# Pieces of x sent from ACT's queue, and the first weight tiles asked for ahead of unit 1's loads

## The chip, the cores and the metric

One core of a Trainium2 chip. The metric is the device time of one execution in microseconds; the kernel before takes 977.13 us (median of 3 runs, 976.09 to 979.07).

## What is computed

A gated linear attention over 4 batches, 8 heads, 768 steps and heads of 48, then two MLPs, from 384 to 2048 and back, over the 3072 tokens:

```python
state = zeros((B, H, D, D))
for t in range(S):
    state = alpha[:, :, t, :, None] * state + einsum('bhd,bhe->bhde', k[:, :, t], v[:, :, t])
    y[:, :, t] = einsum('bhd,bhde->bhe', q[:, :, t], state)
x = y.transpose(0, 2, 1, 3).reshape(B * S, H * D)      # 3072 x 384
h = x @ w_in1
x = where(h >= 1, h, where(h <= -1, 0, (h + 1) ** 2 / 4)) @ w_out1
h = x @ w_in2
out = (h * cos(h)) @ w_out2
```

The weights are float64, read as pairs of 32-bit words. The kernel rebuilds a float32 from each pair and splits it in a high and a low fp32r half.

## The kernel before, in words

**Tiling.** The tokens form 8 units of 384 (half a batch each), the heads 4 pairs. `attention(m)` handles one pair of one unit (32 in all), in chunks of 128 steps; pair 3 of a unit comes first, then 0, 1 and 2. It loads alpha, k and q ("token loads", line 465 for units 0 and 1, line 473 for later ones) and v (line 431 for unit 0, line 492 later), turns them (TensorE for units 0 and 1, line 531; DVE later, line 519), scans alpha forward and backward on DVE (lines 561 and 593), makes masked scores (lines 689 and 699), chunk states (`ks` copied by ACT at line 653 or carried through DRAM, the outer products at line 721, scaled by ACT at line 782 into `kf` and `T`, advanced by DVE at line 792) and y (lines 746 and 751). ACT writes the high half of the result (`high`, line 830), DVE or for four pairs POOL the low half (lines 844 and 838).

**The pieces of x.** The MLP wants 384 rows as 3 tiles of 128, but a pair has 2 x 48 rows in a tile. The result of the first pair of a unit goes to a staging tile `stg`; from there pieces of 16 rows, two transfers for each of the other three pairs, are sent into the free rows of their tiles (`fragments`, line 852). That makes 24 pairs of transfers, 48 KB each, and all of them are issued by SP. `step1` of a unit waits for them.

**The weights.** `weight(layer, kind, f)` fetches a raw tile (lines 326, 329, 339 and 340), then ACT scales (line 352, `wy`), DVE rebuilds (lines 356, 360 and 366, `wz`), ACT makes the high half (line 377) and POOL the low one (line 381). In layer 1 two tiles of w_in are fetched together, 288 + 96 KB twice, and a tile of w_out is 384 KB. Raw buffers: two slots for pairs of w_in, two for w_out. 32 tiles of layer 1 are kept in SBUF, and all units use them.

**The MLPs.** `step1` does for a unit and one of the 16 slices of 128 hidden columns: h (9 matmuls, line 888) into one of two `h` banks, relu by ACT (line 966, or lines 978 to 984), two operations by DVE (lines 970 and 974, or 992), the high half of g by ACT (line 919), its low half by POOL (line 924), and 9 matmuls into acc. `step2` does the same with h cos h. In the units 0 and 1 the turning of tokens uses the `h` banks too.

**What sets the order.** `Order` is a planner that runs while the kernel is built. Every operation is added with its engine, an assumed duration, the operations that it comes after, its buffers, a latency `lat` for those behind it and a `span` that counts in its priority (its `tail`: the longest sum of spans behind it; without a `span` the duration counts). The planner takes the engine whose next operation can start first by its own model, and of those ready at that time the one with the largest tail. It emits the instructions in that order, and each engine runs its own in order. SP and ACT are engines among the others: an issue of a transfer takes its place in the queue of the engine that it is given to, with its wait. `SPREAD` gives the pairs' results a span.

Of the kernel before, what the change touches and what calls it, by code (L numbers as in the profile page):

```python
# [37 lines left out]
Q_DVE = (0, 1, 2, 3, 4, 6)  # L38
TURN = 2
MERGED = 0  # L40
LOW_POOL = (25, 28, 30, 31)
ALPHA_BANK = "sc"
ACT_STEPS = ((4, 10, 12, 15), (1, 4, 10, 14))
# [23 lines left out]
class Order:  # L67
# [7 lines left out]
    def buf(self, tag):  # L75
        b = Buf(tag)
        b.seq = self.made[tag] = self.made.get(tag, -1) + 1
        return b

    def add(self, eng, dur, fn, after=(), new=(), use=(), span=None, lat=None):  # L80
        lat = LATENCY.get(eng, 0.0) if lat is None else lat
        op = Op(len(self.ops), eng, dur, fn, [], list(new), dur if span is None else span, lat)
        for b in new:
            b.first = op
        for b in (*new, *use):
            b.users.append(op)
        op.after = list({id(x): x for x in (*after, *(b.first for b in use)) if x is not None}.values())
        for x in op.after:
            x.next.append(op)
        op.need = len(op.after)  # L90
        self.ops.append(op)
        return op
# [64 lines left out]
def gla_two_mlps(  # L157
# [21 lines left out]
    nc = tc.nc  # L179
# [3 lines left out]
    NP = H // 2  # L183
# [37 lines left out]
    add, buf = o.add, o.buf  # L221
# [5 lines left out]
    def dve(n):  # L227
        return n / 960 + 0.07
# [4 lines left out]
    def pool(n):  # L233
        return n / 960 * 2.5 + 0.04 if n > 100 else n / 400 + 0.1
# [7 lines left out]
    HW2, HW3, SWDMA, LOAD = 0.475, 0.65, 1.02, 2.0  # L242
# [44 lines left out]
    pair_of = {}  # L287

    def weight(layer, kind, f, after=()):
# [15 lines left out]
        new = not joint or f % 2 == 0  # L305
        rb = buf(tag) if new else pair_of["buf"]
# [76 lines left out]
        hb, lb = buf(f"w{kind}hi"), buf(f"w{kind}lo")  # L383
        if new:
            cost = 3.4 if joint else 1.6
            pair_of["op"] = add("sp", cost, fetch, after, new=[rb], lat=LOAD + 1)
        a = pair_of["op"]
        a = add("act", act(n, 0.09), scale, [a], new=[yb], use=[rb])
        a = add("dve", dve(n), shift, [a], new=[zb], use=[yb])
# [3 lines left out]
        lo = add("pool", pool(n), rest, [hi], new=[lb], use=[zb, hb])  # L393
# [6 lines left out]
    X1OPS = {}  # L400
# [6 lines left out]
    v0_ops = []  # L407
    v0b = buf("x2_0")
    chain = [None]

    def early_buffers():

        for _ in range(2):
            xb, t = buf("x"), {}

            def take(t=t):
                t[0] = xp.tile([P, 8, 2, CH * D], F32, tag="x", name="raw0")

            add(None, 0.0, take, new=[xb], lat=0.0)
            xraw.append((xb, t))  # L420
        add(None, 0.0, None, new=[v0b], lat=0.0)
        b, t = buf("x2_2"), {}

        def take_second():
            t[0] = x2p.tile([P, 6, N], F32, tag="x2_2", name="second")

        add(None, 0.0, take_second, new=[b], lat=0.0)
        xraw.append((b, t))
        for c in range(CH):
            def load(c=c):  # L430
                nc.sync.dma_start(
                    v0[:, c, :, 0:D], v[0, :, c * C:(c + 1) * C, :].rearrange("h p d -> p h d")
                )
            v0_ops.append(add("sp", 1.0, load, use=[v0b], lat=LOAD + 1))

    def attention(m):
        u, j = pairs[m]
# [13 lines left out]
        loads, rawb = [], []  # L451
        for x, src in enumerate((alpha, k, q)):
            i = 3 * m + x
            in_x = turned and i < 16
            rb = xraw[i // 8][0] if in_x else buf("raw")

            def load_tokens(x=x, src=src, i=i, rb=rb, in_x=in_x):

                if in_x:
                    dst = xraw[i // 8][1][0][:, i % 8]  # L460
                else:
                    dst = raw_b[rb.slot][:, 0:2 * CH * D].rearrange("p (e x) -> p e x", e=2)
                d["raw", x] = dst.rearrange("p e x -> p (e x)")
                off = ((b * H + 2 * j) * S + s0) * D
                nc.sync.dma_start(dst, bass.AP(src.tensor, off, [[CH * D, P], [S * D, 2], [1, CH * D]]))

            def load(e, z, x=x, src=src, rb=rb):

                d["raw", x] = dst = raw_b[rb.slot]
                off = ((b * H + 2 * j + e) * S + s0) * D + 32 * z  # L470
                n = R * D - 32 * z
                p0 = 64 * e + 32 * z
                nc.sync.dma_start(dst[p0:p0 + 32, 0:n], bass.AP(src.tensor, off, [[R * D, 32], [1, n]]))  # L473

            if not in_x:
                add(None, 0.0, None, new=[rb], lat=0.0)
            if turned:
                loads.append([add("sp", 0.7, load_tokens, use=[rb], lat=LOAD)])
            else:
                loads.append([  # L480
                    add("sp", HW2, lambda e=e, z=z, f=load: f(e, z), use=[rb], lat=LOAD)
                    for e in range(2) for z in range(2)
                ])
            rawb.append(rb)
# [252 lines left out]
        def within_and_before(cs):  # L737

            def fn():
                if cs[0] == 0:  # L740
                    yb.tile = ps(tag_y)
                for c in cs:
                    s = slice(c * C, (c + 1) * C)
                    t = state[c][0]
                    for e, z in enumerate((slice(0, 64), slice(64, K))):
                        nc.tensor.matmul(  # L746
                            yb.tile[z, s], lhsT=vcols(c, z), rhs=am_b[amb.slot][:, e, s], start=True, stop=t is None
                        )
                    if t is not None:
                        for e, z in enumerate(hrows):  # L750
                            nc.tensor.matmul(  # L751
                                yb.tile[z, s], lhsT=state_of(t)[:, e, :], rhs=d["tq"][0:K, s], start=False, stop=True
                            )

            known = [x for c in cs for x in state[c] if x is not None]
            done.append(
                add(
                    "pe",
                    0.15 + 0.235 * sum(1 if state[c][0] is None else 2 for c in cs),
                    fn,  # L760
                    [*masks, *v_ops[:cs[-1] + 1], *(x for x in known if isinstance(x, Op))],
                    new=[yb] if cs[0] == 0 else [],
                    use=[amb, vb, qb, *(x for x in known if isinstance(x, Buf))] + ([yb] if cs[0] else []),
                )
            )

        for c in range(CH):
            start = s0 == 0 and c == 0
            state[c] = (None, None) if start else (T[j], T_OP[j])
            if u < MERGED:  # L770
                within_and_before([c])
# [36 lines left out]
        first, late = j == NP - 1, early and j == NP - 2  # L808
# [5 lines left out]
        xb, stb = X1B[u]  # L814
# [33 lines left out]
        def fragments(js):  # L848
            def fn():
                for jj in js:  # L850
                    for i in range(2):
                        nc.sync.dma_start(
                            x1["x"].bitcast(F32)[64 * i + D:64 * i + 64, jj],
                            x1["stg"].bitcast(F32)[64 * i + 16 * jj:64 * i + 16 * jj + 16],
                        )
            return fn
# [8 lines left out]
            new=[stb] if first else [xb] if makes else [],  # L865
            use=[yb] + ([] if first or makes else [xb]),
        )
        if m in LOW_POOL:
            ycb = buf("ta")
            a = add("act", act(N), copied, [hi], new=[ycb], use=[yb])  # L870
            lo = add("pool", k_ * pool(N), low_pool, [a], use=[ycb, stb if first else xb])
        else:
            lo = add("dve", k_ * dve(N), low, [hi], use=[yb, stb if first else xb])
        X1OPS[u].append(lo)
        X1OPS.setdefault((u, "first"), lo)
        if early and first:
            add(None, 0.0, new_x1, new=[xb], lat=0.0)
            X1OPS[u].append(add("sp", 2 * HW3, fragments([NP - 2]), [lo], use=[xb, stb], lat=LOAD))
        elif not first and not late:
            X1OPS[u].append(add("sp", 2 * HW3, fragments([j]), [lo, X1OPS[u, "first"]], use=[xb, stb], lat=LOAD))  # L880
        chain[0] = add(None, 0.0, None, [X1OPS[u][-1], None if first else chain[0]], span=SPREAD.get(u, SPREAD[None]), lat=0.0)
        X1OPS[u].append(chain[0])
        GLA_END.append(lo)
# [262 lines left out]
    steps = [(u, f, f == a, f == b - 1, a > 0) for u, a, b in segs for f in range(a, b)]  # L1146

    early_buffers()
    for m in range(len(pairs)):
        attention(m)  # L1150
    judge()
    for f in range(FT):
        weight(1, "in", f)
        weight(1, "out", f)
    for s in steps:
        step1(*s)
    for f in range(FT):
        weight(2, "in", f, after=GLA_END[-1:])
        weight(2, "out", f, after=GLA_END[-1:])
# [195 lines left out]
```

## Time and profile before

| | |
|---|---|
| median of 3 runs | 977.13 us (976.09 to 979.07) |
| profiled execution | 979.92 us, its span 978.1 us |
| TensorE busy | 943.6 us (96%) |
| DVE busy | 592.0 us (61%) |
| ACT busy | 580.9 us (59%) |
| POOL busy | 427.1 us (44%) |
| mean granted TensorE clock | 0.993 of full speed |
| transfers | all issued by SP, 70.62 MB on its queue |

The engines' busy time counts no issue of a transfer; these stand in the rows of the queues (SPq). Matmuls are pipelined and their ends are modelled, so a busy TensorE is not at its peak all the time. A wait is put down to the one that came last. The attention of all units and the first MLP fill the span until about 500 us, the second MLP the rest.

### The profile page before, as it was taken

The numbers are of one execution on the slowest core, as the hardware profiler recorded it, in microseconds if no ns is written. First come the engines' busy times: TensorE is split into PE (matmuls) and PEld (weight loads), VectorE is DVE, ScalarE is ACT, GpSimd is POOL, SyncE is SP. The second block draws the span as 40 slices with busy tenths as digits, with TensorE's granted clock in tenths as the row PEclk, the third lists the DMA queues.
The fourth block names the chain that finished last, engine by engine and source line by source line (L and its number), as shares of the span: only waits on it lengthen the run. The fifth ranks groups of instructions, "written<-read, shape, count | busy, mean of one in ns | idle before, by whom it ended". The sixth has DMA issues, their size and how long they took to land.

```text
span 978.1 us, 17438 instructions
## 1 busy us (share of the span) xinstructions
PE 943.6 (96%) x6186; PEld 902.2 (92%) x6186; DVE 592.0 (61%) x1237; ACT 580.9 (59%) x1318; POOL 427.1 (44%) x464
## 2 busy tenths in 40 slices
PE   7779989999999999999999999999999999999997
PEld 5658878899999999989999999999999999999996
DVE  5789899788868677676446896333333333333332
ACT  3657666544545444544445698666666666666664
POOL 2246565555334334443336686434342434243322
PEclk9899999999999999999999999999999999999999
DMA  7677585334645334342132451000000000000000
GB/s 163 126 166 146 140 178 133 76 76 110 138 99 108 91 76 113 74 115 52 21 118 79 133 160 34 25 1 25 1 25 1 25 1 25 1 25 1 25 1 28
DMA packets 113552, 71.82 MB, mean 73 GB/s; under 512 B 71728, under 2 KB 96304, under 8 KB 113456
## 3 DMA queue, kind: packets, MB, share of 16 engines
q1 hardware_dynamic: 113456, 70.62, 30.5%
q8 instruction: 50, 0.82, 0.4%
q14 instruction: 46, 0.38, 0.1%
HBM read 58.79 MB, written 9.44 MB: 70 GB/s over the span
## 4 chain that ended last, share of the span: by engine, by line
PE 84%; DVE 6%; DMA 3%; ACT 2%; issue 2%; SPq 2%; POOL 0%; DVEq 0%; POOLq 0%; ACTq 0%
PE acc L888 33%; PE h L888 27%; PE sc L888 5%; PE kv L888 5%; PE y L888 5%; PE y L746 2%; PE sc L689 2%; PE h L531 2%; PE y L751 1%; PE kv L721 1%; DVE wz L356 1%; DMA raw<-in_alpha_dram 1%; DMA w_raw<-in_moe_w_in_dram 1%; SPq L473 1%; DMA ks<-scr 1%
## 5 line engine op out<-in xcount | busy, mean ns | idle before, releaser
L924 POOL TENSOR_TENSOR gl<-ang,gh 128x384 fp32r<-128x384 f32 x127 | 128.8, 1014 | 233.9 <-ACT gh L919 208.4
L924 POOL TENSOR_TENSOR gl<-r,gh 128x384 fp32r<-128x384 f32 x128 | 131.8, 1030 | 172.1 <-ACT gh L919 138.0
L888 PE MATMUL h<-x,winhi 128*128 128x384 f32 x768 | 198.6, 339 | 6.2 <-DVE r L974 3.1
L888 PEld LDWEIGHTS h<-x,winhi 128*128 128x128 f32 x768 | 137.8, 188 | 10.4 <-DVE r L974 3.9
L888 PE MATMUL acc<-gh,wouthi 128*128 128x384 f32 x384 | 135.8, 354 | 0.0
L888 PE MATMUL acc<-gl,wouthi 128*128 128x384 f32 x384 | 130.0, 338 | 0.3 <-POOL gl L924 0.3
L888 PE MATMUL acc<-gh,woutlo 128*128 128x384 f32 x384 | 130.0, 339 | 0.0
L888 PE MATMUL h<-x,winlo 128*128 128x384 f32 x384 | 129.0, 336 | 0.6 <-POOL winlo L381 0.5
L966 ACT ACTIVATE r<-h,half 128x384 f32<-128x384 f32 x120 | 69.7, 581 | 96.7 <-PE h L888 95.7
L970 DVE TENSOR_TENSOR h<-r,h 128x384 f32<-128x384 f32 x120 | 67.3, 561 | 83.6 <-ACT r L966 83.2
L919 ACT CAST gh<-r 128x384 fp32r<-128x384 f32 x128 | 65.6, 512 | 79.4 <-DVE r L974 71.6
L1077 ACT ACTIVATE ang<-ang 128x384 f32<-128x384 f32 x128 | 67.2, 525 | 61.8 <-DVE ang L1072 61.8
L888 PE MATMUL h<-x2s,winhi 128*128 128x384 f32 x402 | 103.0, 337 | 0.0
L919 ACT CAST gh<-ang 128x384 fp32r<-128x384 f32 x128 | 65.7, 513 | 55.8 <-DVE ang L1084 55.8
L888 PE MATMUL acc<-wouthi,gl 128*128 128x384 f32 x288 | 97.4, 338 | 0.3 <-POOL gl L924 0.3
L888 PE MATMUL acc<-wouthi,gh 128*128 128x384 f32 x288 | 96.9, 337 | 0.0
L888 PE MATMUL acc<-woutlo,gh 128*128 128x384 f32 x288 | 96.9, 336 | 0.0
L1084 DVE SCALAR_TENSOR_TENSOR ang<-ang,h 128x384 f32<-128x384 f32 x67 | 37.1, 554 | 67.6 <-ACT ang L1080 67.5
L888 PEld LDWEIGHTS acc<-gh,wouthi 128*128 128x128 f32 x384 | 71.9, 187 | 6.5 <-issue 2.8
L888 PEld LDWEIGHTS h<-x2s,winhi 128*128 128x128 f32 x402 | 73.4, 188 | 0.0
L888 PEld LDWEIGHTS h<-x,winlo 128*128 128x128 f32 x384 | 72.1, 188 | 1.2 <-POOL winlo L381 1.2
L888 PEld LDWEIGHTS acc<-gl,wouthi 128*128 128x128 f32 x384 | 72.1, 188 | 0.8 <-POOL gl L924 0.8
(167 smaller groups left out, 2118.7 us busy)
## 6 DMA issues: line engine op xcount, KB each, us to landing
w_raw<-in_moe_w_out_dram SPq DMA_DIRECT2D x18, 384.0 KB, 3.4
scr<-G SPq DMA_DIRECT2D x96, 48.0 KB, 1.8
ks<-scr SPq DMA_DIRECT2D x24, 192.0 KB, 2.7
out_dram<-o SPq DMA_DIRECT2D x24, 192.0 KB, 1.9
v<-in_v_dram SPq DMA_DIRECT2D x56, 72.0 KB, 2.6
w_raw<-in_moe_w_in_dram SPq DMA_DIRECT2D x10, 384.0 KB, 3.5
raw<-in_alpha_dram SPq DMA_DIRECT2D x48, 72.0 KB, 2.1
raw<-in_k_dram SPq DMA_DIRECT2D x48, 72.0 KB, 2.0
```

Of the source, the lines that this page charges most:

```text
L356: nc.vector.tensor_scalar(out=t["z"], in0=t["y"], scalar1=3, scalar2=None, op0=ALU.logical_shift_left)
L473: nc.sync.dma_start(dst[p0:p0 + 32, 0:n], bass.AP(src.tensor, off, [[R * D, 32], [1, n]]))
L531: nc.tensor.transpose(bank.tile[0:n, c:N:CH], d["raw", x][:, f0:f0 + n], ident)
L689: nc.tensor.matmul(x.tile[:, s], lhsT=d["tk"][z, s], rhs=d["tq"][z, s], start=True, stop=True)
L746: nc.tensor.matmul(yb.tile[z, s], lhsT=vcols(c, z), rhs=am_b[amb.slot][:, e, s], start=True, stop=t is None)
L888: nc.tensor.matmul(o, lhsT=lhs[a], rhs=rhs[b], start=first and i == 0, stop=last and i == 2)
L919: nc.scalar.copy(ghb.tile, g())
L924: eng.tensor_tensor(out=glb.tile, in0=g(), in1=ghb.tile, op=ALU.subtract)
L966: nc.scalar.activation(rb.tile, h.tile[:, 0:N], AF.Relu, bias=half, scale=0.5)
L970: nc.vector.tensor_tensor(out=hh, in0=rb.tile, in1=hh, op=ALU.max)
L1077: nc.scalar.activation(rb.tile, rb.tile, AF.Sin, scale=HALF_TURN)
L1084: nc.vector.scalar_tensor_tensor(out=rb.tile, in0=rb.tile, scalar=1.0, in1=h.tile[:, 0:N], op0=ALU.subtract, op1=ALU.mult)
```

## The change

The pieces of x are sent by ACT's queue instead of SP's (`nc.scalar.dma_start`), and the planner has them as operations of ACT of twice 0.475 us (`HW2`) instead of twice 0.65 us on SP. Three kinds of loads get a larger span: the fetches of the first w_in pair and of the first two w_out tiles (`f < W_SOON` in layer 1), and unit 0's v loads 4000 more, and the token loads of the first four pairs (unit 0) 8000 more. The durations and latencies of the loads stay as they are.

```diff
+SOON = 4000.0
+W_SOON = 2
+U_SOON = 4
...
             cost = 3.4 if joint else 1.6
-            pair_of["op"] = add("sp", cost, fetch, after, new=[rb], lat=LOAD + 1)
+            pair_of["op"] = add(
+                "sp", cost, fetch, after, new=[rb], span=cost + SOON * (layer == 1 and f < W_SOON), lat=LOAD + 1
+            )
...
-            v0_ops.append(add("sp", 1.0, load, use=[v0b], lat=LOAD + 1))
+            v0_ops.append(add("sp", 1.0, load, use=[v0b], span=1.0 + SOON, lat=LOAD + 1))
...
             if turned:
-                loads.append([add("sp", 0.7, load_tokens, use=[rb], lat=LOAD)])
+                loads.append([add("sp", 0.7, load_tokens, use=[rb], span=0.7 + 2 * SOON * (m < U_SOON), lat=LOAD)])
...
                 for jj in js:
                     for i in range(2):
-                        nc.sync.dma_start(
+                        nc.scalar.dma_start(
                             x1["x"].bitcast(F32)[64 * i + D:64 * i + 64, jj],
                             x1["stg"].bitcast(F32)[64 * i + 16 * jj:64 * i + 16 * jj + 16],
                         )
...
         if early and first:
             add(None, 0.0, new_x1, new=[xb], lat=0.0)
-            X1OPS[u].append(add("sp", 2 * HW3, fragments([NP - 2]), [lo], use=[xb, stb], lat=LOAD))
+            X1OPS[u].append(add("act", 2 * HW2, fragments([NP - 2]), [lo], use=[xb, stb], lat=LOAD))
         elif not first and not late:
-            X1OPS[u].append(add("sp", 2 * HW3, fragments([j]), [lo, X1OPS[u, "first"]], use=[xb, stb], lat=LOAD))
+            X1OPS[u].append(add("act", 2 * HW2, fragments([j]), [lo, X1OPS[u, "first"]], use=[xb, stb], lat=LOAD))
```

## Rows read from the trace of the kernel before

**Rows 1.** The page's busy times: us, share of the span, instructions.
```profile
PE 943.6 (96%) x6186; PEld 902.2 (92%) x6186; DVE 592.0 (61%) x1237; ACT 580.9 (59%) x1318; POOL 427.1 (44%) x464
```
**Rows 2.** Stretches: length, busy PE, PEld, DVE, ACT, POOL; clock, DMA share, GB/s.
```profile
0.00:10.00 10.00, 5.14 (x23) 4.08 (x24) 3.65 (x12) 2.89 (x6) 4.46 (x24) 1.00 0.92 185
10.00:20.00 10.00, 9.47 (x70) 7.42 (x70) 6.05 (x18) 3.95 (x13) 1.29 (x3) 1.00 0.75 185
20.00:30.00 10.00, 8.79 (x98) 7.10 (x99) 8.03 (x22) 5.89 (x18) 1.26 (x3) 1.00 0.69 125
30.00:67.00 37.00, 27.20 (x290) 22.66 (x287) 28.46 (x78) 24.19 (x67) 12.13 (x14) 0.86 0.64 136
67.00:120.00 53.00, 49.23 (x324) 45.06 (x325) 47.11 (x93) 34.22 (x82) 33.23 (x33) 1.00 0.71 150
120.00:200.00 80.00, 74.00 (x494) 67.20 (x492) 69.24 (x137) 49.94 (x116) 44.83 (x45) 1.00 0.54 120
200.00:500.00 300.00, 298.64 (x2217) 279.01 (x2217) 214.05 (x475) 143.88 (x357) 125.27 (x141) 1.00 0.40 89
```
**Rows 3.** Groups of instructions, 0 to 200 us: DVE's rebuilding of the weights.
```profile
L356 DVE TENSOR_SCALAR wz<-wy 128x384 int32<-128x384 int32 x32 | 19.9, 636 | 1.7 <-ACT wy L352 1.6
L360 DVE SCALAR_TENSOR_TENSOR wz<-wy,wz 128x384 int32<-128x384 int32 x32 | 18.6, 600 | 0.0
...
L366 DVE SCALAR_TENSOR_TENSOR wz<-w_spare,wz 128x384 uint32<-128x384 uint32 x16 | 12.5, 801 | 0.0
...
L366 DVE SCALAR_TENSOR_TENSOR wz<-w_raw,wz 128x384 uint32<-128x384 uint32 x16 | 10.2, 639 | 0.0
```
**Rows 4.** Chain of waits, 20 to 36 us: start, us, what.
```profile
19.98 0.49 ACT stg L830
20.49 0.41 DVE stg L844
...
25.53 5.68 DMA w_raw<-in_moe_w_in_dram
```
**Rows 5.** ACT's timeline ahead of 47 us: start, us, operation [idle before].
```profile
21.63 0.48 ACT L539 COPY tk<-h 112x384 f32<-112x384 f32 x1 [1.17 <-PE h L531]
...
31.37 0.54 ACT L352 ACTIVATE wy<-w_raw 128x384 f32<-128x384 f32 x1 [2.45 <-DMA w_raw<-in_moe_w_in_dram]
...
45.09 1.26 ACT L782 ACTIVATE kf<-kv,fe 48x48 f32<-48x48 f32 x4 [2.04 <-PE kv L721]
```
**Rows 6.** Waits of SP's queue, 0 to 60 us: total, times, longest.
```profile
SPq L852 <- DVE x L844: 9.7, 1, 9.7
SPq L852 <- DVE am L699: 6.5, 2, 6.0
```
**Rows 7.** SP's queue in order of time: start, us, transfer, count.
```profile
9.78 0.47 SPq L465 DMA_DIRECT2D raw<-in_alpha_dram  x1
...
21.08 1.24 SPq L852 DMA_DIRECT2D x<-stg  x2
...
44.69 1.15 SPq L852 DMA_DIRECT2D x<-stg  x2
```
**Rows 8.** TensorE's timeline ahead of 37 us.
```profile
14.70 0.88 PE L721 MATMUL kv<-v,ks 128*64 128x48 f32 x12 [0.53 <-ACT ks L653]
...
29.44 1.48 PE L531 MATMUL h<-ident,raw 128*112 128x128 f32 x12
...
33.47 0.55 PE L721 MATMUL kv<-v,ks 128*64 128x48 f32 x12 [2.26 <-ACT ks L653]
...
36.42 0.87 PE L721 MATMUL acc<-v,ks 128*64 128x48 f32 x12 [1.54 <-ACT am L702]
```
**Rows 9.** All instructions of line 852: duration in ns, min/median/max.
```profile
L852 SPq DMA_DIRECT2D x<-stg x48: 507/546/619, 21.1 to 496.2; - x48
```
**Rows 10.** ACT's waits, 200 to 500 us: total, times, longest.
```profile
ACT r L966 <- PE h L888: 79.7, 63, 3.4
```
**Rows 11.** TensorE's waits, 200 to 500 us, all that there are.
```profile
PE kv L721 <- DMA ks<-scr: 1.4, 2, 1.1
```

## The prediction

> **What bounds the kernel now.** I read the page's busy times first: TensorE is busy 943.6 of 978.1 us [rows 1], so at most 34.5 us can be won without taking work away. The table by stretches [rows 2] says where those lie: TensorE is idle 4.86, 0.53 and 1.21 us in the first three tens of us, 9.80 from 30 to 67, 3.77 from 67 to 120, 6.00 from 120 to 200 and only 1.36 from 200 to 500. The granted clock is 1.00 in all of these but from 30 to 67, where it is 0.86: part of that stretch ran at 1.2 instead of 2.4 GHz. So this change, which acts on loads and on ACT, can win only ahead of 200 us; from 200 to 500 it can nearly only lose.
>
> Ahead of 67 us no engine is full: the attention of units 0 and 1 is a chain through TensorE, DVE, ACT and POOL. From 67 to 200 DVE is the fullest beside TensorE (47.11 of 53 and 69.24 of 80 us), much of it with the rebuilding of the weights: 32 tiles by 200 us, three operations each, 19.9 + 18.6 + 12.5 + 10.2 = 61.2 us, or 1.91 us a tile [rows 3].
>
> Next the chain of waits [rows 4]. It runs from ACT's high half of `stg` (ended at 20.47) over DVE's low half to SP, which stands at the first piece of x (line 852) until 21.08, and on through SP's queue: a k load, a v load and the first weight tiles follow there. The last of the first pair's four transfers goes out at 25.53 and takes 5.68 us to land, at 31.2. In ACT's timeline [rows 5] the in-order `wy` operation has kept ACT idle for 2.45 us by then. SP's waits give the size of its stands ahead of 60 us: 6.5 us at line 852 with the first piece, and 9.7 us with a later one [rows 6], which SP's queue shows to be the one of 44.69 [rows 7].
>
> **Part 1: the first weights earlier.** By the new priorities the 12 token loads of unit 0 go out first, then the three v loads, then one pair of w_in tiles (4 transfers) and two w_out tiles (2), then unit 1. Issues of 0.47 us and a little between them [rows 7] put v at about 6.9 us, the weights at about 9 and unit 1 at about 12, where its first load went out at 9.78. The transfers set the landing: 12 x 144 + 576 + 768 + 768 KB at 185 GB/s, the rate of both first tens of us [rows 2], bring v by 12.8 us, the w_in pair by 17.0 and the second w_out tile by 21.3 (estimates from these rows). So the first weights come some 14 us ahead of 31.2. Who is made to wait: v is first read at 14.70, a margin of 1.9; unit 1's first load, by the same sum due at about 22, is read at 29.44, a margin of 7 [rows 8]. I cost both at nothing; if that cover goes, each us past it is a us on the chain.
>
> *What goes:* TensorE's stalls of 2.26 and 1.54 us ending at 33.47 and 36.42, both for ACT's copies [rows 8]. All 3.80 is the upper bound, nothing the lower (the wait may only move). What is late next at 33.47 is the copy itself, some 0.5 us after TensorE's last operation; ACT's am copy stands behind T and kf scalings too, so about half of the second stall stays: 1.7 + 0.8 = 2.5. As the chain behind is also freed of ACT's `wy` operations, I take **3.0**, between 2.5 and 3.8.
>
> *What DVE gains:* between 17 and 30 us DVE is idle about 0.3 x 3.95 + 1.97 = 3.2 us [rows 2], in which it can now rebuild weights that it rebuilds after 67. TensorE is idle 9.8 us from 67 to 200, not all of it for DVE, so this is worth 0 to 3.2; I take half, **1.6**. More can't move: each kind of raw buffer has two slots, and a refill waits for DVE's last read as before.
>
> **Part 2: pieces from SP to ACT.** There are 24 pairs, 48 transfers of 0.507 to 0.619 us of issue, median 0.546 [rows 9]: about 1.09 us a pair and 26 us in all off SP. After 200 us SP's queue is hardly anybody's last wait: TensorE waits 1.4 us for `ks<-scr` and for no other transfer [rows 11]. Bounds 0 to 1.4; I take **0.6**.
>
> What ACT pays isn't in the trace, since no transfer goes out from ACT. Its bounds are nothing (it issues beside a running ACTIVATE) and all 24 x 1.09 = 26 us on the path; I take SP's 1.09 as the occupation, the nearest row, and ask what hides it. Of the first three pairs the first, ready at 21.08, pushes ACT's copy of 21.63 by up to 0.5 us, which other idle time of ACT ahead of 30 us takes up (5.89 of 10 busy [rows 2]); the second falls in what was the 2.45 us of idle; the third, ready at 44.69, delays the kf scalings of 45.09 [rows 5] by about 0.7, on the chain. From 200 to 500 ACT is idle 1.27 us on average ahead of its relu (79.7 us, 63 times [rows 10]), which hides 1.09. So I take a loss of **0.8**, the third pair and a little.
>
> The Trainium skill ("Perfetto Trace Analysis", section "DMA Instruction — HWDGE (DVE, Sync)") says that the issuing sequencer locks the descriptor generator for exclusive use and is free for its next instruction only when the descriptors are made. By that ACT's next instruction stands behind every piece, and the loss would lie nearer to the upper bound than 0.8; no run here shows it yet.
>
> **Sum:** 3.0 + 1.6 + 0.6 - 0.8 = 4.4 us. Against the profiled execution that is 979.92 - 4.4 = 975.5; it stood 2.8 above the median of the runs, so the prediction for the median is 977.13 - 4.4 = **972.7 us**. The runs of this kernel lie up to 3.0 us apart, so 0.3% (2.9 us) is about what a measurement can tell from no change.
>
> **Rivals.** *Clock regained (faster still).* If the stretch from 30 to 67 has fewer stalls and stays at 2.4 GHz, its 27.20 us of TensorE work shrinks to 0.86 of it [rows 2], another 3.8 us: 968.9. Against it: TensorE doesn't bound that stretch, so a shorter matmul is mostly a longer wait.
>
> *The wait only moves (no change).* The DMA engines are 0.92 and 0.75 busy in the first 20 us [rows 2]. What is put ahead pushes the rest back; v has only 1.9 us of margin, and a late v stops the same chain. If the 3.0 us are lost so, 977.13 - 1.6 - 0.6 + 0.8 = 975.7. Against it: the 0.75 falls in SP's stand at line 852, when there was room for the weights.
> The Trainium skill ("DMA: Bandwidth & Descriptors", section "Issuing engines are not separate DMA queues") has it that transfers started by several engines run on the same DMA engines and that only the issue time is saved. By this rule the change would win just the first pair's 1.24 us in SP's chain [rows 7], 975.9; the 6.5 and 9.7 us in [rows 6] say that here an in-order wait is saved too.
>
> *ACT stands behind the pieces (slower).* Place: ACT's queue in units 1 to 7, 21 pairs, between the high half and the next relu. A piece put right behind the high half waits about 0.6 us for the low half (20.47 to 21.08 [rows 4, 7]) and then issues for 1.09: 1.69 us against 1.27 of idle ACT, 0.42 over, 21 times 8.8 us. It decides once the relu is late by more than TensorE's two h banks cover; the copies of g are queued behind it, and TensorE waits for those. Time: 977.13 - 5.2 + 0.8 + 8.8 = 981.5. For it: TensorE has no idle from 200 to 500 to absorb it. Against it: the order is planned with ACT's occupation in it, so other operations can be put between.
>
> **Chances.** Forecast 0.45, with its own range from all gains at their ends (3.8 + 3.2 + 1.4 = 8.4, so 968.7) to 974.2, where 0.3% begins; clock regained 0.12; wait moved 0.22; ACT late 0.21. The whole order is planned anew from the priorities, which scatters each case by some us. So the range goes from 965.0 to the slow case's own 981.5 and leaves out that case's far half and a little below. Faster 0.57, the same 0.22, slower 0.21.
>
> **What would show it.** Right: weights asked for at about 9 us and landed by 17 to 21; no wait of ACT for `w_raw` near 31; TensorE idle from 30 to 67 down from 9.8 to about 6.8, from 67 to 200 from 9.8 to about 8; still under 2 from 200 to 500. Wrong: a wait of TensorE for v near 14.7 or for unit 1's tokens near 29; relus pushed back behind line 852, with TensorE's waits for the results above 2 us between 200 and 500; DVE as full as before from 120 to 200 with TensorE idle as before.

## The result, and the profile after

The changed kernel takes **988.07 us** (median of 4 runs, 987.89 to 989.62) against 978.10 for the kernel before beside it (976.09 to 980.28): a ratio of 1.011, 95% interval 1.0085 to 1.0136. It is 1.1% slower; the forecast was 972.7, with a range up to 981.5. The profiled execution took 988.02 us, its span 986.2, against 979.92 and 978.1. Lines below the edited ones have moved by 3 to 5: 852 is now 857, 888 is 893, 1020 is 1025.

The page's busy times, which answer to [rows 1]:

```profile
PE 944.6 (96%) x6186; PEld 902.4 (92%) x6186; DVE 592.5 (60%) x1237; ACT 578.3 (59%) x1318; POOL 426.5 (43%) x464
```

Stretches of the changed kernel, which answer to [rows 2], and one more behind them:

```profile
0.00:10.00 10.00, 5.08 (x23) 4.33 (x24) 3.65 (x12) 2.89 (x6) 4.47 (x24) 1.00 0.81 201
10.00:20.00 10.00, 8.54 (x95) 6.74 (x93) 7.26 (x23) 6.55 (x19) 1.38 (x3) 1.00 1.15 227
20.00:30.00 10.00, 8.16 (x95) 6.61 (x94) 9.39 (x28) 5.74 (x18) 1.19 (x2) 1.00 0.82 176
30.00:67.00 37.00, 28.54 (x294) 24.18 (x295) 32.92 (x80) 25.34 (x70) 14.62 (x18) 0.91 0.70 143
67.00:120.00 53.00, 50.46 (x333) 47.59 (x332) 48.93 (x96) 34.45 (x79) 33.18 (x32) 0.97 0.67 144
120.00:200.00 80.00, 71.09 (x472) 65.58 (x471) 61.99 (x127) 47.03 (x112) 43.07 (x43) 0.96 0.45 108
200.00:500.00 300.00, 295.66 (x2179) 274.30 (x2178) 212.19 (x469) 140.85 (x351) 122.74 (x138) 0.99 0.42 94
500.00:740.00 240.00, 237.82 (x1348) 234.97 (x1347) 129.58 (x252) 161.53 (x345) 121.08 (x121) 1.00 0.17 53
```

One line of the kernel before, beside which the last of these stands:

```profile
500.00:740.00 240.00, 240.00 (x1371) 239.98 (x1370) 131.32 (x254) 166.20 (x352) 122.61 (x123) 1.00 0.19 59
```

Subtract TensorE's busy time from each length and compare with [rows 2]. Idle time goes up by 1.6 us in the first 30, down by 1.3 from 30 to 67 and by 1.2 from 67 to 120, up by 2.9 from 120 to 200, by 3.0 from 200 to 500, and by 2.2 from 500 to 740, where the kernel before had none. That is 7.1; TensorE's busy time is 1.0 longer; together the 8.1 us between the spans. A gain is where it was forecast, but a smaller one; 1.6 us of the loss lie ahead of it and the rest behind it.

The largest single stand from 120 to 200, in TensorE's timeline (start, us, operation, idle before and what ended it):

```profile
154.49 0.69 PE L893 MATMUL acc<-gh,wouthi 128*128 128x384 f32 x1 [6.30 <-DVE x L1025]
154.98 0.52 PE L893 MATMUL acc<-gl,wouthi 128*128 128x384 f32 x1
...
157.49 0.34 PE L893 MATMUL acc<-gh,wouthi 128*128 128x384 f32 x1
```

TensorE stands 6.30 us because DVE has not yet copied the finished accumulator into x, and behind that stand the matmuls take 0.52 us in place of 0.34 until about 157.4: the granted clock of 150 to 160 us is 0.66, so part of it ran at 1.2 instead of 2.4 GHz. DVE's timeline shows why the copy is late:

```profile
147.40 0.32 DVE L797 SCALAR_TENSOR_TENSOR T<-T,fe,kf 112x96 f32<-112x96 f32 x1 [1.14 <-ACT kf L787]
147.63 1.22 DVE L598 TENSOR_TENSOR_SCAN G<-sc,fe,big 112x127 f32<-112x127 f32 x3
...
149.22 1.35 DVE L369 SCALAR_TENSOR_TENSOR wz<-w_raw,wz 128x384 uint32<-128x384 uint32 x1
...
153.90 0.54 DVE L1025 COPY x<-acc 128x384 f32<-128x384 f32 x1
```

From 147.4 on DVE doesn't wait, it works through scans, weights and turned tokens that its in-order list puts ahead of the copy.

The waits of SP's queue, whole span (total, times, longest). The trace of before has none of this kind:

```profile
SPq L478 <- DMA x<-stg: 9.2, 5, 4.7
SPq L497 <- DMA x<-stg: 5.2, 2, 2.9
SPq L342 <- DMA x<-stg: 4.4, 1, 4.4
SPq L470 <- DMA x<-stg: 4.3, 2, 3.4
```

SP waits 23.1 us, in 10 waits, for pieces that it no longer sends: token loads, v loads and a weight fetch stand behind them. In the kernel before SP stood at the pieces themselves, at line 852, 63.0 us in 22 waits. So its waits for pieces have become fewer, but they now stand ahead of other transfers. In SP's queue the wait of the weight fetch shows as a hole between two transfers of one tile:

```profile
132.22 0.43 SPq L343 DMA_DIRECT2D w_spare<-in_moe_w_in_dram  x1
137.05 0.31 SPq L342 DMA_DIRECT2D w_spare<-in_moe_w_in_dram  x1
```

From 200 to 500, TensorE's waits (compare [rows 11]):

```profile
PE kv L726 <- issue: 2.4, 2, 2.0
PE kv L726 <- DMA raw<-in_q_dram: 1.5, 1, 1.5
PE kv L726 <- PE h L893: 0.4, 1, 0.4
```

A q load is late there, for which TensorE didn't wait before.

### The profile page after: what moved, and what is told of

The parts are those of the page before. It is cut to its first block, busy times and chain, and to the rows that moved or that the text cites. A ratio compares the mean times of both kernels' runs of the same rounds, so it can differ in the third digit from the quotient of the medians.

```text
span 986.2 us, 17413 instructions
## 1 busy us (share of the span) xinstructions
PE 944.6 (96%) x6186; PEld 902.4 (92%) x6186; DVE 592.5 (60%) x1237; ACT 578.3 (59%) x1318; POOL 426.5 (43%) x464
## 4 chain that ended last, share of the span: by engine, by line
PE 77%; DVE 5%; ACT 3%; issue 1%; SPq 1%; DMA 0%; POOL 0%; DVEq 0%; ACTq 0%
PE acc L893 31%; PE h L893 27%; PE kv L893 5%; PE sc L893 5%; PE y L893 4%; PE y L751 2%; PE sc L694 2%; PE y L756 1%; PE kv L726 1%; DVE wz L359 1%; DVE ang L1077 1%; DVE wz L369 0%; ACT ang L1082 0%; ACT gh L924 0%; SPq L478 0%
## 5 line engine op out<-in xcount | busy, mean ns | idle before, releaser
L893 PE MATMUL acc<-gh,wouthi 128*128 128x384 f32 x384 | 137.8, 359 | 6.6 <-DVE x L1025 6.3
```

Source lines behind the costliest of these rows:

```text
L893: nc.tensor.matmul(o, lhsT=lhs[a], rhs=rhs[b], start=first and i == 0, stop=last and i == 2)
```

## The experiments

Fifteen kernels, in four groups (e1 to e4, e5 to e8, the n's and the o's), each group on a chip of its own; each ratio is to runs of the kernel before beside them on the same chip. "Plan" is the list of operations that `Order` sorts; "issue" is the engine whose queue sends the piece. The two can be set apart.

### The change taken in parts

**e1: the weights early, the pieces left on SP** (plan and issue):

```diff
-                        nc.scalar.dma_start(
+                        nc.sync.dma_start(
...
-add("act", 2 * HW2, fragments(...
+add("sp", 2 * HW3, fragments(...
```

> The pieces go back to SP (in the planner too), the larger spans of the first loads stay. Shared counters (the eight completion semaphores are taken in turn by the transfers of both queues, so an SP transfer waits for a piece that stands in ACT's queue): the loss was the pieces', so this is 971 to 977 us, SP waits for no x<-stg transfer, TensorE idle from 120 to 200 us below 6. New order (each change of the plan scatters the time, the queue has no part in it): anywhere from 972 to 988. Early weights at fault: 984 to 990, with a stall of TensorE over 4 us somewhere from 120 to 200.

Measured: 973.42 us (971.99 to 976.78), ratio 0.9961, 0.9944 to 0.9978. Stretches of this kernel:

```profile
30.00:67.00 37.00, 29.87 (x309) 24.63 (x307) 33.95 (x84) 26.84 (x73) 19.37 (x20) 0.95 0.74 157
67.00:120.00 53.00, 49.49 (x325) 45.40 (x324) 47.38 (x98) 33.77 (x78) 31.15 (x31) 1.00 0.68 149
120.00:200.00 80.00, 75.30 (x514) 68.72 (x515) 70.20 (x139) 49.63 (x118) 46.71 (x47) 1.00 0.46 107
```

TensorE's idle time is 7.1 us from 30 to 67 and 8.2 from 67 to 200; the prediction wrote 6.8 and 8. This half of the change gains, and it is the one version below both kernels.

**e2: the pieces alone on ACT** (plan and issue), the larger spans of the loads taken out:

```diff
-                        nc.sync.dma_start(
+                        nc.scalar.dma_start(
...
-add("sp", 2 * HW3, fragments(...
+add("act", 2 * HW2, fragments(...
```

> The kernel before with the pieces on ACT (in the planner too), the spans as before. Shared counters: 983 to 990 us, SP waits 10 us or more in total for x<-stg transfers, and one of these waits ends in a stall of TensorE of 2 us or more. New order: anywhere from 972 to 988, whatever SP waits for. Early weights at fault: 975 to 980.

Measured: 989.62 us, ratio 1.0116 (1.0086 to 1.0147). The pieces alone cost as much as the whole change; SP's waits for `x<-stg` sum to 33.3 us.

**e3: the order of before, and only the issue moved to ACT:**

```diff
-                        nc.sync.dma_start(
+                        nc.scalar.dma_start(
```

> Order of the kernel before, planned with the pieces on SP, and only their issue is moved to ACT's queue at the same place in time; TensorE and DVE have the same instructions in the same order as before. Shared counters: SP waits 10 us or more for x<-stg transfers and the time is 980 to 986. New order: the order is the same, so 976 to 980. ACT stands behind the pieces: 980 to 990, with ACT's waits or its issue ahead of the late relus and no SP wait behind it.

Measured: 982.78 us (979.91 to 984.63), ratio 1.0056 (1.0038 to 1.0074). Every other engine has before's order, so these 5.5 us (982.78 - 977.29) are the queue's. TensorE is busy 71.27 us from 120 to 200 there, where before had 74.00 [rows 2]. The waits of SP's queue for pieces:

```profile
SPq L473 <- DMA x<-stg: 19.4, 8, 6.6
SPq L340 <- DMA x<-stg: 8.2, 2, 5.1
SPq L465 <- DMA x<-stg: 1.8, 1, 1.8
```

and one of them in SP's queue, where the issue of three token loads is drawn out to 7.86 us:

```profile
70.47 7.86 SPq L473 DMA_DIRECT2D raw<-in_alpha_dram  x3
```

Another can be followed to TensorE. One transfer of a weight tile stands 5.16 us, until a piece that ACT sends at 142.76 has landed, and the transfers behind it go out late with it:

```profile
141.28 0.42 SPq L339 DMA_DIRECT2D w_spare<-in_moe_w_in_dram  x1
146.86 0.31 SPq L340 DMA_DIRECT2D w_spare<-in_moe_w_in_dram  x1
...
153.16 0.38 SPq L673 DMA_DIRECT2D ks<-scr  x1
```

In the kernel before this `ks` load goes out at 149.39 and TensorE doesn't wait for it. Here it does:

```profile
156.34 0.52 PE L721 MATMUL kv<-v,ks 128*64 128x48 f32 x12 [2.02 <-DMA ks<-scr]
```

The program's list of instructions tells why SP waits (number in the engine's list, line, transfer, what it waits for). The first two are ACT's, the others SP's:

```
13 L852 DMA x1_136<-stg_305 16x768 [waits DMAHW7_49,DVE_49]
14 L852 DMA x1_136<-stg_305 16x768 [waits DMAHW1_49]
...
28 L339 DMA w_raw_107<-in_moe_w_in_dram 48x3x512 [waits DMAHW5_49]
29 L340 DMA w_raw_107<-in_moe_w_in_dram 16x3x512 [waits DMAHW6_49]
30 L339 DMA w_raw_107<-in_moe_w_in_dram 48x3x512 [waits DMAHW0_49]
31 L340 DMA w_raw_107<-in_moe_w_in_dram 16x3x512 [waits DMAHW2_49]
```

SP's and ACT's transfers take turns on eight completion counters, and a transfer that comes to a counter waits until the one that had it last has landed. Counters 7 and 1 went to pieces in ACT's queue, so a later load of SP that comes to 7 or 1 has to wait until ACT has reached its piece and the piece is there. The other way nothing of size shows: 7.0 us of ACT's waits, three of them, are put down to landings of `x<-stg`, but those are ACT's own pieces.

**e4: the changed kernel's order, the issue back on SP:**

```diff
-                        nc.scalar.dma_start(
+                        nc.sync.dma_start(
```

> Order of the changed kernel, planned with the pieces on ACT, and only their issue is put back on SP's queue; TensorE and DVE have the same instructions in the same order as in the changed kernel. Shared counters: SP waits for no x<-stg transfer, the wait of 6.3 us of TensorE for DVE's x copy near 148 us falls to 3 or less, 977 to 982 us. New order: that wait stays above 5 us, 986 to 990. ACT stands behind the pieces: ACT's 26 us of issue are gone and the time falls to 977 to 982 without any change in SP's waits.

Measured: 989.45 us (988.3 to 994.3), ratio 1.0138 (1.0104 to 1.0172). Nothing comes back, and the counters' range of 977 to 982 is missed. With SP issuing in both, e4 and e1 differ only in how the pieces are planned (the engine and its assumed time), and lie 16 us apart. The stand on line 1025 is there too, 6.53 us long at 153.63.

### Counters and late copy

**e5: the order of before, the pieces issued by POOL**, whose transfers use counters of their own:

```diff
-                        nc.sync.dma_start(
+                        nc.gpsimd.dma_start(
```

> Order of the kernel before for TensorE, DVE and ACT, as in e3_order_before, but the pieces are issued by POOL, whose transfers have completion counters of their own. Shared counters (e3's 5.5 us came from SP and ACT waiting for each other's pieces through the eight shared counters): SP waits for no x<-stg transfer, TensorE's wait of 2.0 us for ks<-scr is gone, 976 to 980 us. In-order queue (what costs in e3 is that a computing engine's queue stands behind a piece): POOL stands in the same way, 981 to 986 us.

Measured: 978.46 us, ratio 0.9996 (0.9979 to 1.0014). SP has no wait for `x<-stg`, and TensorE's wait of 2.0 us for `ks<-scr` is gone. Against e3 the counters and the issuing engine differ, and the 5.5 us are gone; POOL pays nothing that shows. So 2.0 us of e3's loss are followed from one of SP's waits to TensorE. I read the rest as theirs too, but that isn't shown: what ACT's own standing at its pieces adds, e3 and e5 don't separate. e5 also measures what SP gains when it is freed of the pieces, all 63.0 us of standing at them included: nothing (978.46 against 978.26).

**e6 and e7: the kernel before, with another assumed issue time for a piece on SP**, 0.60 and 0.70 us for 0.65. Nothing but the planner's order changes:

```diff
-HW2, HW3, SWDMA, LOAD = 0.475, 0.65,
+HW2, HW3, SWDMA, LOAD = 0.475, 0.60,
```

> The kernel before, only the planner's assumed issue time of a piece is 0.60 us for 0.65, so nothing but the order changes. DVE's copy of the first accumulator into x, which TensorE waits for near 148 us in the changed kernel, stands 12 places later in DVE's order here than before (251 for 239, as in the changed kernel). Late copy: 982 to 988 us with a stall of TensorE of 4 us or more for this copy. Pieces' queue: 976 to 979, as the queue is the same.

> As e6_scatter_a with 0.70 us, the copy again at place 251. Late copy: 982 to 988 us with a stall of TensorE of 4 us or more for this copy. Pieces' queue: 976 to 979.

Measured: 987.14 us (ratio 1.0092, 1.0071 to 1.0114) and 982.26 us (1.0045, 1.0021 to 1.0069). A changed guess of 0.05 us costs 4 to 9 us. Both times are in the range of the late copy, and both kernels have its stand of TensorE at line 1020, 6.99 us in e6 and 4.1 us in e7: a late copy goes with lost time, also with the pieces on SP. The order of before is a good one among its neighbours.

**e8: the changed kernel, with the copies of the accumulator into x put first in the priorities:**

```diff
         for op in self.ops:
+            op.tail += op.boost
...
             X2OPS[u, c] = [p]
+            p.boost = 4000.0
```

> The changed kernel, with the copies of the accumulators into x (and the additions to it) preferred by the planner over everything else that is ready; the copy stands at place 215 of DVE's order for 251. Late copy: the 6.3 us of TensorE near 148 us are gone, 976 to 983 us (what is left is the pieces on ACT). Pieces' queue: 985 to 990, the stall turns up elsewhere.

Measured: 990.68 us, ratio 1.0121 (1.0099 to 1.0142). The 6.3 us stand is gone and the time is not: from 67 to 200 TensorE now waits 3.0 us for `am`, 2.9 for `sc`, 1.7 for `F` (all DVE's) and 1.5 for POOL's `tk`. So in this order the late copy was the form that the loss took, and without it the loss takes others.

### Is it that one order, or every order with the pieces on ACT?

**n1 and n2: the changed kernel, a piece assumed to take ACT 0.60 and 0.55 us** in place of 0.475 (the diff is n1's):

```diff
-add("act", 2 * HW2, fragments(...
+add("act", 2 * 0.6, fragments(...
```

> The changed kernel (pieces planned and issued on ACT, spans kept), with one literal of the plan altered: a piece is assumed to take ACT 0.60 us of issue in place of 0.475. In this order the copy of the first accumulator into x stands at place 185 (pair before) and 232 of DVE's order, in the changed kernel at 251. Theory A (the late copy near 154 us is most of the loss): no 6 us stall of TensorE on DVE x near 154, and 973.4 plus the 5.5 of the shared counters = 979, between 976 and 982. Theory B (pieces on ACT make any such plan slow): 986 to 990 whatever the place.

> As n1_act_60, with 0.55 assumed; the copy stands at place 257 of DVE's order, later than in the changed kernel (251). Theory A: the stall of TensorE on DVE x near 154 us is there, 5 to 8 us long, and the time is 986 to 990. Theory B: 986 to 990. Only n1 tells A from B; a time under 982 here speaks against A.

Measured: 992.72 us (ratio 1.0174, 1.0146 to 1.0202) and 994.22 us (1.0189, 1.0161 to 1.0217). Theory A falls with n1: its copy, at place 232, holds TensorE for 2.0 us only, and it is slower still. TensorE's timeline, first of n1, then of n2:

```profile
115.45 0.58 PE L694 MATMUL sc<-tq,tk 48*128 48x128 f32 x1 [8.24 <-POOL tk L615]
```

```profile
162.05 0.69 PE L893 MATMUL acc<-gh,wouthi 128*128 128x384 f32 x1 [5.13 <-DVE x L1025]
```

The long stand changes its place and its releaser from order to order.

**n3 and n4: e1 with 0.60 and 0.70 us assumed for a piece on SP** (the diff is n3's, against e1):

```diff
-add("sp", 2 * HW3, fragments(...
+add("sp", 2 * 0.6, fragments(...
```

> The weights asked early, the pieces left on SP (e1_priorities), and a piece assumed to take SP 0.60 us in place of 0.65. Copy at place 240 of DVE's order, as in e1_priorities. Theory A: 973.4 within 2 us, no stall on DVE x near 154. If the gain of e1_priorities was only a lucky order: anywhere from 973 to 985.

> As n3_sp_60 with 0.70 assumed; the copy stands at place 252. Theory A: TensorE stands 4 to 7 us on DVE x near 150, and the time is 973.4 + 4 to 10 = 977 to 984. Theory B (only pieces on ACT cost): 973.4 within 2 us, as no piece is on ACT.

Measured: 977.45 us (ratio 1.0004, 0.9988 to 1.0021) and 978.39 us (1.0010, 0.9990 to 1.0030). n4 has its stand of 4.3 us on line 1025, as foreseen, yet lies only 0.9 above n3, which has 1.5 us there. And e1 is the best of its three: its gain of 3.9 us is no more than the 4.0 and 5.0 us by which its neighbours lie above it.

### What the plan charges

**o1: the changed kernel's plan with the pieces on SP at almost no time, issued by SP:**

```diff
-add("act", 2 * HW2, fragments(..., lat=LOAD)
+add("sp", 0.02, fragments(..., span=2 * HW3, lat=LOAD)
```

> The changed kernel's plan with the pieces again among SP's operations and issued by SP, but assumed to take it 0.02 us in place of 2 x 0.65 (their span in the priorities kept). The plan then charges neither SP nor ACT for them. Theory F (the slow orders come from the plan no longer charging SP, so that SP's other loads are asked for earlier than the chip can): 986 to 994. Theory C (they come from charging ACT with 2 x 0.475): 972 to 980. Theory N (each order falls where it falls): anywhere from 973 to 990, and the three runs show no pattern.

Measured: **1016.71 us** (1015.17 to 1019.05), ratio 1.0389 (1.0347 to 1.0431), above even the range of theory F. Against e1 (973.42) nothing differs but the assumed time of a pair, 0.02 for 1.3 us. From TensorE's timeline, and two stretches:

```profile
109.96 0.58 PE L694 MATMUL sc<-tq,tk 48*128 48x128 f32 x1 [5.09 <-POOL tk L615]
...
122.97 0.74 PE L726 MATMUL kv<-v,ks 128*64 128x48 f32 x11 [11.29 <-DVE wz L359]
...
128.94 0.58 PE L694 MATMUL sc<-tq,tk 48*128 48x128 f32 x1 [2.73 <-POOL tk L615]
...
142.64 0.69 PE L893 MATMUL acc<-gh,wouthi 128*128 128x384 f32 x1 [11.97 <-DVE x L1025]
```

```profile
67.00:120.00 53.00, 35.74 (x237) 31.86 (x235) 49.00 (x97) 30.42 (x72) 26.68 (x28) 0.85 0.71 154
120.00:160.00 40.00, 22.33 (x127) 21.30 (x128) 27.90 (x56) 16.34 (x41) 18.91 (x20) 0.64 0.61 144
```

TensorE is idle 17.3 and 17.7 us in these two stretches, with DVE 49.00 of 53 us busy in the first: stands of the kind that the changed kernel has, one of them for line 1025 too, and larger. The granted clock is 0.64 in the second.

**o2: e1, with an empty operation of ACT's beside each piece**, so that the plan charges both engines:

```diff
+X1OPS[u].append(add("act", 2 * HW2, None, [lo], lat=0.0))
 X1OPS[u].append(add("sp", 2 * HW3, fragments(...
```

> The weights asked early, the pieces planned and issued on SP at 2 x 0.65 (e1_priorities, 973.4), and besides an empty operation of 2 x 0.475 us on ACT in the plan beside each of them, which emits nothing. Theory F: 972 to 980. Theory C: 986 to 994. Theory N: anywhere from 973 to 990.

Measured: 982.24 us (979.85 to 983.45), ratio 1.0048 (1.0027 to 1.0069): 2 us above F's range and 4 below C's.

**o3: the changed kernel's plan with the pieces on ACT at almost no time, issued by SP:**

```diff
-add("act", 2 * HW2, fragments(..., lat=LOAD)
+add("act", 0.02, fragments(..., span=2 * HW2, lat=LOAD)
```

> The changed kernel's plan with the pieces among ACT's operations at 0.02 us in place of 2 x 0.475, and issued by SP. The plan charges neither engine. Theory F: 986 to 994. Theory C: 972 to 980. Theory N: anywhere from 973 to 990.

Measured: **1010.23 us** (1009.99 to 1010.67), ratio 1.0327 (1.0287 to 1.0368), again above all three ranges.

Together, by what the plan charges for a pair of pieces (medians in us; e3 and e5 have before's order in other queues and are left out):

| charged to | kernels and times |
|---|---|
| SP alone | e1 973.4, n3 977.5, before 977.1, n4 978.4, e7 982.3, e6 987.1 |
| SP and ACT | o2 982.2 |
| ACT alone | changed kernel 988.1, e4 989.5, e2 989.6, e8 990.7, n1 992.7, n2 994.2 |
| neither | o3 1010.2, o1 1016.7 |

Every kernel whose plan doesn't charge SP is slower than every one whose plan does, if only by 0.9 us for the nearest two (e6 and the changed kernel), which weren't timed side by side and whose ratios overlap (1.0071 to 1.0114, 1.0085 to 1.0136). Theory C falls: with ACT's charge taken away the kernel gets slower by 21 us (e4 to o3), not faster. What the slow rows have in common is that SP isn't charged, and where that alone is changed, from e1 to o1, it costs 43 us, three times what orders differ by within a row. Within a row orders differ by up to 14 us.

## Why the prediction was wrong, point by point

**Part 1, the first weights, was right in its direction and place; its size isn't settled.** SP's queue in the changed kernel:

```profile
9.51 0.89 SPq L342 DMA_DIRECT2D w_raw<-in_moe_w_in_dram  x1
...
12.34 0.43 SPq L329 DMA_DIRECT2D w_spare<-in_moe_w_out_dram  x1
12.81 0.43 SPq L470 DMA_DIRECT2D raw<-in_alpha_dram  x1
```

The weights are asked for from 9.5 us and unit 1 from 12.8, where the text had about 9 and 12, and TensorE waits neither for v nor for unit 1's tokens. ACT's first `wy` starts at 17.97 where it was 31.37 [rows 5], after a wait of 0.30 us, and the wait near 31 is gone; one of 2.0 us for a w_out tile comes between 60 and 120. Measured by itself (e1) this half gives 977.29 - 973.42 = 3.9 us, where the text had 3.0 + 1.6 = 4.6. How much of the 3.9 belongs to the order that came out isn't settled, as n3 and n4 give nothing over before; but the place fits, from 30 to 67. Against it stand 0.8 us more of idle TensorE in e1's first 30 us, which the text had at nothing. In the changed kernel itself TensorE is idle 8.5 us from 30 to 67, 11.5 from 67 to 200 and 4.3 from 200 to 500, where the signs wanted 6.8, 8 and under 2.

**Part 2, the pieces, is the step that failed: "Bounds 0 to 1.4; I take 0.6" for SP, and "a loss of 0.8" for ACT.** Together they make a loss of 0.2 us. The pieces alone cost 12.3 (e2, 989.62 - 977.29), and their queue alone 5.5 (e3). Both terms looked at the occupation of the two sequencers, and that was sized about rightly. The trace of the changed kernel, all pieces on ACT's queue (duration in ns, least, median, most):

```profile
L857 ACTq DMA_DIRECT2D x<-stg x48: 514/598/1014, 20.5 to 500.9; - x48
```

598 ns stands beside SP's 546 [rows 9]. The Trainium skill ("Perfetto Trace Analysis", section "DMA Instruction — HWDGE (DVE, Sync)") has the issuing sequencer stand until the descriptors are made; the trace agrees: two pieces sent at 27.26 take ACT 1.16 us, and its next operation starts at 28.47. But the loss isn't there: TensorE's waits from 200 to 500 name no relu and no copy of g, and with the issue back on SP (e4) the time stays. ACT's idle time ahead of its relus, 70.5 us in 54 waits against 79.7 in 63 [rows 10], says only that ACT has a little less slack. What was missed is a third party, SP, which goes on waiting for a piece after it has given it away: 29.4 us of waits in e3, one of which holds up TensorE by 2.0 us. The 0.6 for SP was a choice between its bounds: freed of the pieces, SP gains nothing (e5), and with the counters shared the move loses 5.5. One reading of the text is off as well: of the 6.5 us that it gives to the first piece, [rows 6] has two waits, and that of the first piece is the longer one, 6.0.

**The larger failure is one clause: "The whole order is planned anew from the priorities, which scatters each case by some us."** I took the new order as noise around the sum, even on both sides. It is neither small nor even. Two neighbours of before are 4 and 9 us slower; and with the pieces planned under ACT and charged to it, all five orders tried lie at 988 to 994. From e1 to e4, with the same queue, it is 16 us. This is what decides the sign. In the changed kernel's own order the counters then cost nothing more (e4 989.45, changed kernel 988.07).

**The rivals.** *Clock regained*: the clock from 30 to 67 went from 0.86 to 0.91, with no gain left at the end. In e1, where it went to 0.95, this rival isn't settled. The ten runs of e1 were granted 0.9946 on average, the 17 of the kernel before beside them 0.9920, and among those 17 the two at 0.995 took 975.2 and 975.8 us, the four at 0.990 from 978.0 to 980.4. So part of e1's 3.9 us may be the clock's, which the text had set aside, and that 3.9 lies near 4.6 may be luck. *The wait only moves*, 975.7: the pieces on ACT didn't leave the time where it was. By the Trainium skill ("DMA: Bandwidth & Descriptors", section "Issuing engines are not separate DMA queues") another issuing engine saves issue time and no more, 975.9; e3 shows that it can also cost, 5.5 us. *ACT stands behind the pieces*: its sign came true, at 0.21, by luck: the way was another, and the time lies beyond its 981.5. Its sentence against it, that the order is planned with ACT's occupation in it and so can put other operations between, held too: that planning is where the time went.

**What stays open.** That taking SP's charge out of the plan makes orders slow is shown by e1 and o1 and by the rows of the table. Why, step by step, is shown only in part. Ahead of DVE's first copy of an accumulator into x stand the rebuildings of 25 weight tiles in o1 and o3 (the copy starts at 142.0 and 136.3 us), of 13 in e1 and the changed kernel (86.5 and 92.4). So with neither engine charged, the weights crowd DVE's list. They aren't asked for sooner on the chip: by 100 us SP has sent 33 weight transfers in o1 and in e1. That a plan with SP free takes the loads to land sooner than they do would fit; no run tests it. For the plans that charge ACT alone the step is open. A long stand of TensorE isn't their mark: e2 and e8 have none above 3 us from 67 to 200, and e6 and o2, which charge SP, have 7.0 and 5.8 at the late copy. What all eight kernels without SP's charge share comes later: TensorE is idle 5.7 to 9.8 us from 200 to 740, where all others have 0.9 to 3.9, and from 200 to 500 it waits for a q load, 0.7 to 3.5 us, which none of the others does. e4 and the changed kernel are alike in time, so it is not simply that SP is busier on the chip than in the plan. For o2, one order, 982.2 can be ACT's charge or scatter, so a share of ACT's charge in the loss isn't excluded.

## What to carry to other kernels

Before moving a transfer to another engine's queue, read in the program's list which completion counter it takes and who takes that counter next: a transfer that waits for data can hold up the old queue from the new one. Where a planner makes the order, test the edit of the queue and the edit of the plan apart, as e3 and e4 do, and run two or three neighbours of the order before believing in a gain below 1%: here neighbours lay 1 to 9 us apart. An assumed cost in such a plan also sets the pace of what follows, so making it smaller can make the kernel slower.

## What the runs showed that was not expected

SP waited 23.1 us (changed kernel), 29.4 (e3) and 33.3 (e2) for transfers in ACT's queue, and nothing for the same transfers in POOL's (e5). An assumed issue time of 0.02 in place of 1.3 us in the plan, with the same instructions executed in another order, cost 1016.71 - 973.42 = 43.3 us against e1. And 48 transfers given to POOL left the time as it was, 978.46 against 978.26, where ACT's queue cost 5.5.
